# Column sums of a recurrent memory as four column tiles, with a VectorE transpose for its columns and a new order of TensorE's work

## The chip, the core and the metric

The kernel runs on one core of a Trainium2 chip. The metric is device time in microseconds of one execution of the whole program. Each version is timed several times and the median counts. The profile is of one execution, and its span runs from the first to the last recorded instruction.

The core's engines run in parallel, each through its own list of instructions, and wait for each other by semaphores: TensorE (PE in the profile, its weight loads PEld), VectorE (DVE), ScalarE (ACT), GpSimd (POOL) and SyncE (SP), which issues DMAs.

## What is computed

Four blocks in a row on x of 2048 rows by 448 columns: attention with a recurrent memory, a gated MLP, and both once more, each behind a layer norm and added to x. The attention goes through 64 segments of 32 rows, and the first 8 output rows of each segment are the memory that the next segment sees:

```python
mem = mem0
for s in range(n_seg):                       # 64 segments of 32 rows
    h = jnp.concatenate([mem, xs], axis=1)   # 8 + 32 rows, 448 wide
    q, k, v = h @ Wq, h @ Wk, h @ Wv         # 16 heads of 256
    p = softmax(mask(q @ k.T * scale))
    o = (p @ v) @ Wo                         # 40 rows, 448 wide
    mem = o[:, :M, :]
    outs.append(o[:, M:, :])
```

The MLP is `(relu(x @ W_gate) * (x @ W_up)) @ W_down` with 1792 hidden columns.

## The kernel before

**Products of weights.** At the start Wq and Wk are multiplied into one matrix A per head (`self.A`), Wv and Wo into B (`self.Bsb`), so that a segment needs U = A h, scores = U h, Y = P h and an output product with B only. `product` makes these; the "tails" among them have 64 rows each.

**Shapes of the PE array.** A matmul may use the full array (128*128 in the profile's rows, `mode=0`) or a part of it, a tile, several at a time: four column tiles (128*32, mode 1), two row tiles (64*128 or 40*128, mode 2), two column tiles of 64 (mode 3), or eight tiles 64*32 (mode 4). `packed` makes a full-shape matmul, or in mode 1 four column tiles that together give the same output. The planner has a constant, `TURN = 94.0`, for a change of shape.

**Steps.** `chain(step)` is one step of the recurrence, for both attention layers at once: the second runs `LAG = 7` steps behind the first, which makes 70 steps (0 to 69). In order:

1. `board` and `put` copy rows of other segments into spare columns of `mT` (POOL), where they ride along with the memory's columns. `mT` holds the new memory with its 448 values along the partitions, in seven blocks; keys `MEM` stand for blocks 0 to 3 and `(q, v)` for blocks 4 to 6, which hold the same values with the halves of the partitions exchanged ("cross").
2. U pass: two halves of 56 matmuls, mode 4 (line 1012), out of `mT`; copies to `Usb`, and `turn_u` transposes them on DVE into `uT`.
3. `middle`: scores (line 1208, full shape), softmax, transposed probabilities, Y in `y_part` (mode 2), and a copy to `YTm`.
4. Output pass: 56 matmuls in mode 1 (line 1051), 14 rounds of four column tiles, into one PSUM bank. Each of the four groups of 32 partitions holds a partial sum.
5. `Ohi` (ACT, line 1057) and `Olo` (DVE, line 1058) split that bank into a high and a low bf16 part.
6. Column sums: `cols` adds the four groups of partitions with the 0/1 matrix `Sel`, for both parts: eight full-shape matmuls of 32 columns, with the part of O as weights. The result has the memory's values along the partitions, and is copied to `mT` (DVE line 1074, and two cross copies), which the next step's U pass waits for. A copy `mC` and a DVE transpose (line 1078) make the rows `Rsb` of it.
7. The rows go to HR, for the first layer by POOL or ACT, for the second by DMAs on SP's queue, and those that rode along to `Tsb`.

**The rest of the work** fills the waits of the steps: `att_group` (the 32 rows of each segment that are no memory, a tile of four segments and two pairs of heads at a time: U in mode 2, scores, softmax, Y in mode 2, output products in full shape), the MLP (`glu_units` in mode 2, `glu_down` in full shape), and the norms.

**The order.** The program is a list of operations with their data dependences. `_Sched` gives each an engine and a place. PE's order is written out: `line` reads the string `LINE`, in which each character says how many of the operations still left are passed over. `ORDER` shifts the priority of groups of work on the other engines. Where an operation may take several shapes (`also`), `line` picks one that a stretch of neighbours has in common. `schedule` then plays the order through with estimated times to choose engines and banks, and `emit` writes the instructions and the semaphore waits.

Of the kernel before, what the change touches and what calls it, by code (L numbers as in the profile page):

```python
# [32 lines left out]
ORDER = ("PSaaaaoQzANGSamSAqSOLgAjolycvdUSYubSjbQxCm0psRrSRqEQAEnlIEnOAnPCTSLvPxprWKjnhTaqcrTbZCswsbraAgEaqhIaAGAaALbjaa"  # L33
         "sanTnaBcjaZWzaJKmBaaXOEYXNydtHhPuFSLsyxCuyLuORxJMA0ahaaaFcaCcCvwXmrCfR0DWCgxLBrdmbxaQC0WbaUaEGMqHa0DaosbzhpHdl"
         "WkxycjZaZGxZqQpRM0ymgeScKWuIhXaOAasLNeddFpYkHiTiewgm0WJdepBgztdDKNbipxTsJXOvpslMHKEJoVF00rXwoFGIgKaPjatRPDMuea"
         "g0ocaSMXMaIHQHYDVIDWUiVpGLFgUWXOXqRxiOaWPavfkRxbMdhxgqVYFcSAGpXxSgSAEoXcmvzKKkjJCubDis0XTbcCEuecPXEaPRWQeAORyo"
         "JHhakKaiTmlTpwUptdvkZzUD0fxNPEIziGGTevefmecgNBN0DbQOXaXPaAmfqX0pgSyloPBzIlSQcPTyKhKNWzyvrlHQFAzEIJHKDUe0hkIbfK"
         "e0zD0jsbXGXRaiTdSsamBaeyJqncMKdUTzoxjiugtllgtXxAOALDuUTVXDuwEnupSkNUaUmawjrAwhD0DLNHNtfvqgTZoJlYEDPE0EZYVTJvcw"
         "EWPEtyVNLdZeXmtsDsbxjxMTLchWdCebHajealMjeS0QOmzx0LdAHUaEDleLVrtMnIfHVmwOA0EhlPYqbAQaAoapqAIHThuLPPZmvFxkxWJWwQ"
         "nEPIcOmfgwjXdgAMZuOQkyGNViZI0sZuymZOvStgcYkKYfqeaObatwrfJE0nvRNpbkVuY0SHuqRQoFc0GZT0TAAAfPCDMqpctjaEJaZjWJfdTh"  # L40
         "pHAVWmuFXanPYnQtwEtlLmIiYjsjNpFtBblupwRveZkzOaajmjvuMshnoltlMqsanwaRPeaHaMBoa0oEtmAB0nvHQJTbpphEIqwVCbhqCNIIvN"
         "AaBEaVyVScpWtpFgRMIevwqgYYmNw0vrMkcmKEiy0rhMbriPOmkQrdu0rJkQJhZJIygthcqDsRiWahXPahhdmy0flKddE0aaaaaamLhuKetaaa"
         "aaaaaaaaaaaaaaaajYGwUNxZaCChYbrM")

SIGNS = "ABCDEFGHIJKLMNOPQRSTUVWXYZabcdefghijklmnopqrstuvwxyz0123456789+-*/=<>()[]{}.,:;!"
LINE = ("AAAABAAJAAHHCEDCCBAAIHBADCAAAAAIIEFBBABAAAHICCEAABAAAHIEDAAAAABAIHBAEBCAAAAJHADCBAAAJAAKHGBBCDAAAAfhAfACOABArZ"
        "ABAQVAUDA~QARAQAkPAFMALAAJWABHAGAcAADACARBAbWFBEADPAECMDAEQKGAAPEOOGEAEDAIDCABBDABAAWAAAKAJBAOdAGSAZAEPEEAAAKE"
        "BOACCbbF*FZAAXDGVAUUUAASADCPPAAAMAAKlKsKAJJAIAHHAAFAADACABBBWBBAMSYAAWeAJbUAJILAVKKAAAEEADGAbaGFCCAVFBZBSACQAA"
        "ANNNAAMLALvLA1KQCJIICHHHAHGGGGAcFAAACHCBAAAAXBCAAMAAXXAPGbAHSAXHGAAASDBCDABBBbaEBADCAETZAARCCPAANNNAALAMM54ALJ"
        "sJJCIBHHHAHGAHHeAGADAJDCCAAAAABCAATMBAXWeKcLKTAYMveAtALbKAAAEEAjHTA65GuGCI0C5ABxwAveeFkEqqqIApAAmAEEkkAAAhBmBX"  # L50
        "KdPAba6aaaKJCLWAVWWCAASZSAAAPADNgDQMMMjOGLALLGbJTJAOWAHDZNhGXMMGGGAGQAEAHtsDRHGAnAHAkLoHiGAgggAOAdGAedbAAAZAAd"
        "XAA2VUAAARRRtAQzQRRCDBBABAKAAAHALGFfFFFAHADAAPBCCaZBRLBVbKBZBxIBBBFTHAAXDACDC)(FpFFC[C-ABBD7BA5WCB222AT1AzAAyy"
        "QVdAuUzashqqBgoooACmAlmmMLAiAhMBBkeAdCAAaaaDaKaYQDXXrEpEVAGAYAQQYQWEEOOOHQAALGFY77JAAGA92AFKADxWwOEDtttAFKrApA"
        "qpoENDAkAAJhACf-CCdddeAADaACCZZAAADVbASARuRtRkAQQQGBACBAAKJAWcAAAffmFSdFARQfEE2AACOAYfKNBzBKIMBBBFFBEBA=/EdDC>"
        "9CEZAB4BB2kAaAyyyAyAwRAVuukjzArapEoPADlAAnAiiiJiAgAffDAOUbAgAvZ2Z0ZZZGAaYAWBqAVVD1TCAREAAOTDCqMSMMMPLAADIA33WD"
        "UCzFA3YAvQEDs~HEDqqqGqACnCnnClCCAiADPAAdCBbAeDZZZDDAAVAXWAAATRoRuRWArQEEBCBAAJJJAAAGAATEfYFldEjFEaOAAABbL6KBwB"
        "L1MLBBBLnMLBUEiB=/DACCH8CAB5+A4mED111A1AzUAyyYAAvAbssirQuAZoooADmConAAljBJiAggAACAAfbbbDbFAYZAYYEhDBVAEZAARCPW"
        "PGCNNNAALLKAC+9IPP6AHBA2L6B0RAyyyzPxACxwDUtTCrAREAnIrm;DDkkkAAEhhAihE4DeAdFAAAZCCXAAAAASSSBAhoGCBAABAAIAAAAETZ"
        "gGneSGGRQAAXCDABNYBwBWIBBByIHFBIEAA(>GgFIC-N>CAaB6An4mE222AA0Az10AZxAwA1AdtQ:s.QUApppqAOFBlMllBCAAhAmAIAdAbbSH"
        "GYYYJaEEVAXWACATAAaPWQAOOFBMMMEUATKJA77qQIe3CA7AFzSyZBAvvvAABsAttAAJoQoAAsAAkFii.BAggghD<DDAcAEADDZYAAAVAAASXR"  # L60
        "mRkAQQQCEABCAAJEAWAbAAgTeTlTGAUZAAEDRzayQBMCQLLrCKRBB2K0KBBBAEuPAHDDA44E~XECCCUyCCA1vXAtVsssRQ~CqAPoppBDuPmDAk"
        "ZiBhYAfffXfFBcBdcAAGZBBBcWAUUuDtCFRRRGFAANPAMFMMW2AAaKJDmIdIbDOHHHLLIAFFAvuAOArCAFAnBrAlNCCiiiAiAgDIAeeD{cCAaA"
        "DeAXAWCBATTTAASRASRxQoQAlEAEMALBAAIIIAIDGAUAAYDmmEQbQaQEEAdAVCAN4AAuAKzKAAAEEAsDGA//hGFC9<HdAB5GA3mE111AAzA00A"
        "UAvDvAAty0QrriqqqAZoFOAAAjnmBiiTCMgmAfAddjAAAaaaIHQcXApWaZW)WAWAbAcUMSSG6GGPPPAAONAGWW8GKATAIAQVHDOGNNNOAAAMKA"
        "MMECHJAGAFFaFAEEEAADCAAPAJGbASBAPWDIDIHAJABNBAFCADDBFKAAACCAAAAADBAFAEEFEEEADAC")


class _Op:
    __slots__ = ("idx", "engs", "cost", "fn", "deps", "prio", "dma", "eng", "ndep", "users", "ready",
                 "start", "end", "need_inc", "val", "clock", "slot", "seq", "alloc", "mode",  # L70
                 "touch", "busy", "cross", "at", "also", "land", "side", "group")


class _Bank:
# [9 lines left out]
    def ap(self):  # L84
        return self.psum[self.name][:, :]


class _Sched:
# [14 lines left out]
    LAND = 2400.0  # L103
    ROWS = {"act": 122.0, "dve": 115.0}
# [89 lines left out]
    def line(self):  # L194

        left = [o for o in self.ops if "pe" in o.engs]
        out = []
        k = 0
        for c in LINE:
            if c == "~":  # L200
                k += 80
                continue
            out.append(left.pop(k + SIGNS.index(c)))
            k = 0
        out += left
        run, have = [], None
# [10 lines left out]
    def schedule(self):  # L217
        for o in self.ops:
# [34 lines left out]
        while left:  # L253
# [209 lines left out]
UT = ["uT00", "uT01", "uT10", "uT11"]  # L463
# [91 lines left out]
MEM = [("mT", c) for c in range(2)]  # L555

# [12 lines left out]
class _Kernel:  # L569
# [48 lines left out]
    def alloc(self):  # L618
# [63 lines left out]
        self.Ohi = sb("Ohi", [128, 512])  # L682
        self.Olo = sb("Olo", [128, 512])
        self.mT = sb("mT", [128, 7, 80])
# [23 lines left out]
    def constants(self):  # L708
# [40 lines left out]
        for o in range(4):  # L749
            dve(lambda E, o=o: E.tensor_copy(self.Usb[:, 128 * o:128 * o + 128].rearrange("p (h q) -> p h q", h=H),  # L750
                                             self.ident[:, 8 * o:8 * o + 8].unsqueeze(1).to_broadcast([128, H, 8])),
                r=["ident"], w=[("Usb", o)])
            s.add("pe", 30, lambda E, e, o=o: E.matmul(mb.ap()[:, L * o:L * o + L], lhsT=self.Usb[:, 128 * o:128 * o + 128],
                                                       rhs=self.maskb[:, :], start=True, stop=True),
                  r=[("Usb", o), "mask"], w=[mb], alloc=[mb] if o == 0 else ())
# [3 lines left out]
        pool(lambda E: E.memset(self.YTm[:, :, :], 0.0), w=[("YTm", c) for c in range(2)] + [("YTr", c) for c in range(2)])  # L759
# [3 lines left out]
        pool(lambda E: E.memset(self.Usb[:, :], 0.0), w=[("Usb", r) for r in range(4)])  # L763
        pool(lambda E: E.memset(self.uT[:, 3], 0.0), w=[("uT2", a, b) for a in range(2) for b in range(2)])
        pool(lambda E: E.memset(self.mT[:, :, :], 0.0), w=MEM + ["mTr", "mT3"])
# [18 lines left out]
    def weights(self):  # L784
# [42 lines left out]
        def product(dst, terms, w, mode, scale=None, swap=False):  # L827
# [3 lines left out]
            def fn(E, e):  # L831
                for to, of in ((0, slice(64, D)), (D - 64, slice(0, 64))) if swap else ((0, slice(0, D)),):
                    for et in range(2):
                        for lhs, m0, mn, rhs, row0, _ in terms:
                            i = E.matmul(bk.ap()[row0:row0 + mn, to:to + of.stop - of.start], lhsT=lhs[:, et, m0:m0 + mn], rhs=rhs[:, et, of],  # L835
                                         start=(et == 0), stop=(et == 1), tile_position=(0, row0))
                return i
            s.add("pe", mm_cost(D, D), fn, r=[k for q in terms for k in q[5]], w=[bk], alloc=[bk], room=w, mode=mode)
# [58 lines left out]
        def values(part):  # L897
            for n in range(4 * part, 4 * part + 4):
# [11 lines left out]
                product(self.Bsb[:, b_tail(p), :], tails, [("B", p, hh, 3) for hh in range(2)], 3)  # L910
# [47 lines left out]
    def chain_start(self, c):  # L958
# [8 lines left out]
        for to, of in ((slice(0, 3), slice(0, 6, 2)), (slice(3, 4), slice(7, 8)), (slice(4, 7), slice(1, 6, 2))):  # L967
            s.add("dve", 200, lambda E, e, to=to, of=of: E.tensor_copy(self.mT[:, to, 8 * c:8 * c + 8], self.mT0[:, of, 0:M]), r=["mT0"], w=[("mT", c)], prio=0)
# [14 lines left out]
    def chain(self, step):  # L983
# [11 lines left out]
        late = []  # L995
        if ride:
            self.board(*ride)
        if third:
            u, q, o = third
            self.put(u, slice(q, q + 1), o, 32, "mT3")  # L1000
        first = 8 if third else 0

        for half in range(2):
            ub = [self.bank("C", "G") for _ in range(2)]

            def fn(E, e, half=half, ub=ub):
                for b in range(7):
                    for j in range(4):
                        for v in range(2):
                            rw = slice(64 * v, 64 * v + 64)  # L1010
                            cols = self.A[rw, b, 1792 * half:1792 * half + 1792].rearrange("p (m j i) -> p m j i", j=4, i=32)[:, :, j]
                            i = E.matmul(ub[v].ap()[32 * j:32 * j + 32, 0:D], lhsT=self.mT[rw, WHERE[b], first:first + 32], rhs=cols,  # L1012
                                         start=(b == 0), stop=(b == 6), tile_position=(64 * v, 32 * j))
                return i
# [643 lines left out]
```

## Time and profile before

| | us |
|---|---|
| median of 3 runs | 1483.35 |
| lowest and highest | 1481.13, 1483.98 |
| profiled execution | 1483.32 |
| its span | 1481.4 |
| granted TensorE clock | 1.00 |

A row of the timeline has the start, the time until the last end in it, engine, line, operation, what it writes and from what, and shapes; of a matmul the array shape (rows*columns) comes first, then partitions by columns of the moving operand. Rows of equal operations in a row are merged, with their number (x56). What stands in brackets is the engine's idle time before it and what ended it. The end of a matmul is modelled and has the pipeline's length in it, so the rate of matmuls is read from starts. A row of the stretches has the stretch, its length, then for PE, PEld, DVE, ACT and POOL the busy time and (x) the number of instructions, then the granted clock, the DMA share and GB/s. `L493` is the line in `packed`, which several operations share; their tiles tell them apart (`Sel` for the column sums, `P` for output products of attention or MLP).

### The profile page before, as it was taken

What the parts mean: (1) busy time and instruction counts of PE and PEld (TensorE: products, weight loads), DVE (VectorE), ACT (ScalarE), POOL (GpSimd) and SP (SyncE); (2) the same over time, 40 slices, a digit from 0 to 9 for tenths busy, and PEclk for the clock granted to TensorE, in tenths of its full rate; (3) what the DMA queues carried; (4) which work ended last, traced back from release to release, by engine and by line L of the source; (5) the groups of instructions that cost most, each with busy time, mean ns of one, the idle gap of its engine ahead of it and who ended that gap; (6) DMA issues with size and microseconds to landing.
All of it is one profiled execution on the core that took longest, in us unless ns stands there. A gap on an engine that the chain in (4) does not pass through costs nothing.

```text
span 1481.4 us, 79079 instructions
## 1 busy us (share of the span) xinstructions
PE 1470.8 (99%) x35068; PEld 1040.5 (70%) x35068; DVE 1136.3 (77%) x3743; ACT 925.1 (62%) x2659; POOL 176.0 (12%) x678
## 2 busy tenths in 40 slices
PE   9999999999999999999999999999999999999999
PEld 6556767676767776767768767777667776777676
DVE  6667778788877877687877878587786878688875
ACT  7765757676666666566666656575665656556643
POOL 3010111111110111011110111011110111110000
PEclk9999999999999999999999999999999999999999
DMA  9512100000000000000000000000000000000000
GB/s 267 161 31 66 50 8 9 8 9 8 9 4 16 6 11 11 4 18 4 18 4 11 12 11 12 4 18 5 18 4 11 11 11 12 5 11 5 11 5 15
DMA packets 62246, 33.85 MB, mean 23 GB/s; under 512 B 31809, under 2 KB 61777, under 8 KB 61905
## 3 DMA queue, kind: packets, MB, share of 16 engines
q1 hardware_dynamic: 61584, 28.54, 7.6%
q8 instruction: 276, 4.52, 1.3%
q14 instruction: 66, 0.53, 0.1%
q10 hardware_dynamic: 320, 0.26, 0.1%
HBM read 21.36 MB, written 1.84 MB: 16 GB/s over the span
## 4 chain that ended last, share of the span: by engine, by line
PE 97%; DVE 1%; ACT 1%; issue 0%; DMA 0%; POOL 0%; SPq 0%
PE psG L493 24%; PE psG L1354 17%; PE psC L1051 12%; PE psC L1012 9%; PE psG L1457 9%; PE psG L1012 4%; PE psG L835 3%; PE psG L1266 3%; PE psG L1486 3%; PE psG L1380 3%; PE psC L493 2%; PE psC L1208 1%; PE psC L1266 1%; PE psG L821 1%; PE psG L1051 1%; PE psG L1269 1%
## 5 line engine op out<-in xcount | busy, mean ns | idle before, releaser
L1354 PE MATMUL psG<-HT,A 64*128 64x128 bf16 x4904 | 285.9, 216 | 0.9 <-issue 0.9
L493 PE MATMUL psG<-Bsb,P 128*128 128x448 bf16 x1288 | 276.2, 353 | 0.0
L1354 PE MATMUL psG<-HX,A 64*128 64x128 bf16 x3678 | 267.0, 216 | 0.4 <-issue 0.4
L1354 PEld LDWEIGHTS psG<-HT,A 64*128 64x128 bf16 x4904 | 235.2, 94 | 11.6 <-issue 3.7
L483 ACT ACTIVATE Ug<-psG 64x128 bf16<-64x128 f32 (+2 forms) x447 | 158.9, 372 | 60.0 <-PE psG L1354 43.9
L1354 PEld LDWEIGHTS psG<-HX,A 64*128 64x128 bf16 x3678 | 194.7, 94 | 1.4 <-issue 1.4
L1051 PE MATMUL psC<-Bsb,YTm 128*32 128x448 bf16 x3528 | 178.8, 353 | 0.4
L493 PEld LDWEIGHTS psG<-Bsb,P 128*128 128x128 bf16 x1288 | 110.7, 97 | 94.7 <-issue 11.9
L1012 PE MATMUL psC<-A,mT 64*32 64x448 bf16 x3920 | 152.8, 350 | 0.2
L1012 PE MATMUL psG<-A,mT 64*32 64x448 bf16 x3920 | 152.1, 350 | 0.0
L1192 DVE STREAM_TRANSPOSE uT<-Usb 128x384 bf16<-128x384 bf16 x280 | 144.1, 536 | 0.0
L1051 PEld LDWEIGHTS psC<-Bsb,YTm 128*32 128x32 bf16 x3528 | 88.7, 97 | 70.8 <-issue 2.5
L1457 PE MATMUL psG<-GG,glu 64*128 64x256 bf16 x2352 | 134.2, 269 | 0.0
L1457 PEld LDWEIGHTS psG<-GG,glu 64*128 64x128 bf16 x2352 | 111.9, 94 | 17.0 <-issue 1.9
L486 DVE CAST Ug<-psG 64x128 bf16<-64x128 f32 (+2 forms) x260 | 107.6, 424 | 15.5 <-PE psG L1354 10.7
L1012 PEld LDWEIGHTS psC<-A,mT 64*32 64x32 bf16 x3920 | 78.7, 92 | 57.2 <-ACT mT L483 5.2
L483 ACT ACTIVATE P<-psG 128x448 bf16<-128x448 f32 x210 | 106.4, 545 | 8.6 <-PE psG L1269 7.1
L486 DVE CAST P<-psG 128x448 bf16<-128x448 f32 x148 | 89.1, 614 | 12.7 <-PE psG L1269 11.2
L493 PE MATMUL psG<-glu,P 128*128 128x448 bf16 x448 | 97.6, 352 | 0.0
L1468 DVE TENSOR_TENSOR P<-P,psG 128x512 bf16<-128x512 bf16 x84 | 57.6, 686 | 44.5 <-ACT P L1467 44.0
L1012 PEld LDWEIGHTS psG<-A,mT 64*32 64x32 bf16 x3920 | 79.4, 92 | 17.4 <-issue 0.7
L1058 DVE TENSOR_TENSOR Olo<-psC,Ohi 128x448 bf16<-128x448 f32 x65 | 40.4, 622 | 64.3 <-ACT Ohi L1057 63.8
(253 smaller groups left out, 3025.2 us busy)
## 6 DMA issues: line engine op xcount, KB each, us to landing
HR<-xn SPq DMA_DIRECT2D x128, 32.0 KB, 1.9
Tsb<-Rsb SPq DMA_DIRECT2D x256, 1.5 KB
Tsb<-Rsb SPq DMA_DIRECT2D x256, 2.0 KB
Bsb<-in_A_Wq_dram SPq DMA_DIRECT2D x6, 384.0 KB, 7.3
Bsb<-in_A_Wk_dram SPq DMA_DIRECT2D x6, 384.0 KB, 6.2
HR<-Rsb SPq DMA_DIRECT2D x126, 1.5 KB
HR<-Rsb SPq DMA_DIRECT2D x126, 2.0 KB
X<-in_A_x_dram SPq DMA_DIRECT2D x16, 112.0 KB, 3.1
```

The costliest lines, as they stand in the source:

```text
L483: return E.activation(out, i, ACT.Copy, scale=1.0 if scale is None else scale)
L486: return E.tensor_copy(out, i)
L493: return E.matmul(out, lhsT=lhsT, rhs=rhs, **k)
L835: i = E.matmul(bk.ap()[row0:row0 + mn, to:to + of.stop - of.start], lhsT=lhs[:, et, m0:m0 + mn], rhs=rhs[:, et, of], start=(et == 0), stop ...
L1012: i = E.matmul(ub[v].ap()[32 * j:32 * j + 32, 0:D], lhsT=self.mT[rw, WHERE[b], first:first + 32], rhs=cols, start=(b == 0), stop=(b == 6), ...
L1051: x = E.matmul(bo.ap()[32 * j:32 * j + 32, 0:D], lhsT=self.YTm[:, q, :], rhs=self.Bsb[:, chunks[q], :], start=(i == 0), stop=(i == 13), ti ...
L1192: self.s.add("dve", 560, busy=486.0, fn=lambda E, e, v=v, of=of: E.transpose(outs[:, 2 * v:2 * v + 2], of), r=[("Usb", 2 * half + v)], w=[ ...
L1266: return E.matmul(ps[:, n * q:n * q + n], lhsT=HR[rows, 128 * q:128 * q + 128], rhs=PT, start=True, stop=True, tile_position=(b, 0))
L1354: i = E.matmul(ub[v].ap()[:, 128 * n:128 * n + 128], lhsT=self.A[rw, b, a0:a0 + 128], rhs=HT[rw, WHOLE[b], :, 0:SEG] if CROSS[b] is None e ...
L1380: i = E.matmul(psS()[:, sg, :], lhsT=Ug[:, k, sg, :], rhs=HT[:, k, sg, :], start=(k == 0), stop=(k == 3))
L1457: i_ = E.matmul(two[v].ap()[:, 256 * c:256 * c + 256], lhsT=self.Wgu[rw, b, f0:f0 + 128], rhs=self.GG[rw, :, WHOLE[b] if CROSS[b] is None ...
L1468: s.add("dve", dv_cost(512), lambda E, e, z=z, dst=dst: E.tensor_tensor(dst, dst, z(1), ALU.mult), r=[two[1]], w=w)
```

## The change

In steps 16 to 60 (`EARLY <= step < LATE`) the column sums exchange their operands: `Sel` is the weight, O is streamed, and four column tiles each take one set of 32 columns of every block, for the high part and then the low. Their result has the memory in rows. It is copied to `R`, which was the result of the transpose before, and a DVE transpose of `R` writes the columns straight into `mT`; the cross copies read `mT` in place of PSUM. In the next step the memory stands in columns 16 to 31 of `mT` and what rides along in 0 to 15 (`swap`). The other steps keep the old sums.

```diff
+        if turn:
+            def cols(E, e):
+                for q, O in enumerate((hi_, lo_)):
+                    for j in range(4):
+                        x = E.matmul(br.ap()[32 * j:32 * j + 32, 0:128], lhsT=self.Sel[:, :], rhs=O[:, 64:576].rearrange("p (k i) -> p k i", k=4)[:, :, 32 * j:32 * j + 32],
+                                     start=(q == 0), stop=(q == 1), tile_position=(0, 32 * j))
+                return x
+            s.add("pe", mm_cost(128, 128), cols, r=ok + ["Sel"], w=[br], alloc=[br], room=[rk], mode=1, **P)
+            s.add(EV, ev_cost(128), copy_any(R[:, :], lambda: br.ap()[:, 0:128]), r=[br], w=[rk], **P)
+            s.add("dve", 307, busy=225.0, fn=lambda E, e: E.transpose(self.mT[:, 0:4, m0:m0 + 32], rows), r=[rk], w=MEM + LAST + ["mT3"], **P)
+            for v, (to, of) in enumerate(((low, upp), (upp, low))):
+                s.add(EV, ev_cost(48, fast=True), copy_any(self.mT[to, 4:7, m0:m0 + nm], self.mT[of, 0:3, m0:m0 + nm]), r=MEM, w=xk(v), at=2 + v, side=v, **P)
+        else:
...
-            s.add("pe", mm_cost(*[D] * (hi - lo)), oo, r=yk + bk, w=[bo], alloc=[bo] if (g == 0 and lo == 0) else ())
+            s.add("pe", mm_cost(*[D] * (hi - lo)), oo, r=yk + bk, w=[bo], alloc=[bo] if (g == 0 and lo == 0) else (), also=(1,))
```

The last pair is in `att_group`; the products of `glu_down` and the tails of B get `also=(1,)` in the same way, so that they may be made as four column tiles where a neighbour is. `Ohi` and `Olo` become 576 wide, with the first 64 columns repeated behind the 448 twice instead of once.

The U pass is cut, so that a part may start when the part of `mT` that it reads is there, and in steps 0 to 15 half 1 is copied and transposed in two halves of 224 columns; Y goes to two banks where the first layer alone is running:

```diff
+            split = (((0, 2, 4), MEM), ((1, 3, 5, 6), cross + LAST + LASTX)) if swap else (((0, 2), MEM), ((1, 3), cross), ((4, 5, 6), LAST + LASTX))
+            for bs, mk in split if (early or swap) and half == 0 else whole:
...
+            for gs in ((0,), (1,)) if early and half == 1 else ((0, 1),):
+                n = 224 * len(gs)
...
+        two = len(act) == 1 and c1 == 1 and m["n"] == "m"
+        yb = [self.bank("C", "G") for _ in (0, 1)] if two else [self.bank("C", "G") for _ in act]
```

In the planner, an operation takes the shape of the one behind it where that is its plain shape, and the estimate of PE's time includes a supply of instructions (`FETCH` ns for each, with a lead of at most `AHEAD`):

```diff
+        for a, b in zip(out[-2::-1], out[:0:-1]):
+            if a.mode != b.mode == plain[a.idx]:
+                a.mode = b.mode
...
+                lead = min(self.AHEAD, lead + t0 + c - free[e] - o.ins * self.FETCH[self.FETCH[2] < t0 < self.FETCH[3]])
+                c -= min(lead, 0.0)
+                lead = max(lead, 0.0)
```

`ORDER` and `LINE` are new strings.

More of the change, by code (lines that the diff above doesn't have):

```diff
@@ L1003, in chain @@
+        cross = [(q, v) for q in MEM for v in range(2)]
+        whole = (((0, 1, 2, 3, 4, 5, 6), MEM + cross + LAST + LASTX),)
         for half in range(2):
             ub = [self.bank("C", "G") for _ in range(2)]
[L1006 to L1014, printed above, removed]
@@ L1078, in chain @@
[L1078 removed]
+        low, upp = slice(0, 64), slice(64, 128)
+        nm = 8 if step < LAG else 16
+        ok = [("Ohi", 0), ("Oli", 0), "Oh2", "Ol2"]
+        xk = lambda v: [(q, v) for q in MEM] + [("mTc", v)]
+        br = self.bank("C", "G")
+        rows = R[:, :].rearrange("p (k i) -> p k i", k=4)
+        turn = EARLY <= step < LATE
```

287 lines of the change are left out of this document (171 added, 116 removed).

## The prediction

> **What bounds the kernel now.** I read the page's engine shares and its chain first, then busy time by stretches, then the timeline of one step.
>
> ```profile
> span 1481.4 us, 79079 instructions
> PE 1470.8 (99%) x35068; PEld 1040.5 (70%) x35068; DVE 1136.3 (77%) x3743; ACT 925.1 (62%) x2659; POOL 176.0 (12%) x678
> PE 97%; DVE 1%; ACT 1%; issue 0%; DMA 0%; POOL 0%; SPq 0%
> ```
>
> TensorE is busy for 99% of the span and is 97% of the chain that ended last. The recurrence (70 steps, each using the memory that the step before wrote) isn't what limits the time as long as the order puts other tiles' matmuls into each of its waits. The stretches say where that succeeds:
>
> ```profile
> 0.00:60.00 60.00, 57.93 (x851) 39.31 (x853) 42.62 (x95) 44.51 (x76) 14.37 (x43) 1.00 0.91 260
> 60.00:342.00 282.00, 278.10 (x7018) 190.45 (x7014) 212.27 (x715) 186.75 (x528) 34.96 (x134) 1.00 0.10 25
> 342.00:1262.00 920.00, 918.53 (x22094) 654.36 (x22096) 720.55 (x2418) 576.88 (x1724) 109.48 (x433) 1.00 0.05 10
> 1262.00:1432.00 170.00, 169.82 (x4084) 120.56 (x4069) 131.39 (x440) 99.19 (x291) 16.23 (x67) 1.00 0.04 8
> 1432.00:1481.40 49.40, 46.45 (x1054) 35.86 (x1052) 29.42 (x79) 17.73 (x44) 0.99 (x3) 1.00 0.05 13
> ```
>
> The second number is PE's busy time. From 342 to 1262 us PE idles 1.47 of 920 us: a microsecond of PE work taken out there is a microsecond of the span. These are also, within a step, the steps 16 to 60, for which the change rewrites the column sums. From 60 to 342 us (steps 0 to 15) PE idles 3.9 us. The clock is granted in full (1.00) throughout.
>
> Busy PE time contains more than streaming. One step, from its output pass to the next U pass:
>
> ```profile
> 834.84 2.83 PE L1051 MATMUL psC<-Bsb,YTm 128*32 128x448 bf16 x56
> ...
> 837.60 1.12 PE L493 MATMUL psG<-Bsb,P 128*128 128x448 bf16 x5
> 837.72 0.54 ACT L1057 ACTIVATE Ohi<-psC 128x448 bf16<-128x448 f32 x1 [1.38 <-PE psC L1051]
> ...
> 838.30 0.62 DVE L1058 TENSOR_TENSOR Olo<-psC,Ohi 128x448 bf16<-128x448 f32 x1 [0.67 <-ACT Ohi L1057]
> ...
> 838.62 1.11 PE L493 MATMUL psG<-Bsb,P 128*128 128x448 bf16 x5
> ...
> 838.97 0.17 DVE L1060 COPY Olo<-Olo 128x64 bf16<-128x64 bf16 x1
> ...
> 839.56 0.18 PE L493 MATMUL psC<-Sel,Ohi 128*128 128x32 bf16 x1
> 839.59 0.18 PE L493 MATMUL psC<-Sel,Olo 128*128 128x32 bf16 x1
> ...
> 839.74 0.18 PE L493 MATMUL psC<-Sel,Olo 128*128 128x32 bf16 x1
> ...
> 839.77 0.28 PE L513 MATMUL psG<-ident,Px 128*128 128x64 bf16 x4
> ...
> 839.88 0.92 PE L493 MATMUL psG<-Bsb,P 128*128 128x448 bf16 x4
> 839.96 0.23 DVE L1074 CAST mT<-psC 128x64 bf16<-128x64 f32 x1 [0.81 <-PE psC L493]
> ...
> 840.38 0.20 ACT L483 ACTIVATE mT<-psC 64x48 bf16<-64x48 f32 x1
> ...
> 840.61 0.28 ACT L483 ACTIVATE mC<-psC 128x128 bf16<-128x128 f32 x1
> 840.73 0.09 PEld L1012 LDWEIGHTS psC<-A,mT 64*32 64x32 bf16 x1 [0.37 <-ACT mT L483]
> 840.73 0.36 PE L1012 MATMUL psC<-A,mT 64*32 64x448 bf16 x1
> ...
> 840.75 0.09 PEld L1012 LDWEIGHTS psG<-A,mT 64*32 64x32 bf16 x1
> 840.75 0.36 PE L1012 MATMUL psC<-A,mT 64*32 64x448 bf16 x1
> ...
> 840.92 0.31 DVE L1078 STREAM_TRANSPOSE Rsb<-mC 128x128 bf16<-128x128 bf16 x1 [0.17 <-ACT mC L483]
> 840.93 0.35 PE L1012 MATMUL psC<-A,mT 64*32 64x448 bf16 x1
> ```
>
> The third column of a row (the first number after the time) includes a pipelined tail, so I use differences of start times. Five products of 448 columns in full array shape run from 838.62 to 839.56: 0.188 us each. Four of the same start at 839.88, which should free PE at 840.63, but the U pass, of another array shape (64*32), starts at 840.73: **a change of shape costs 0.10 us**. It is the same at the output pass: 14 sets of four column tiles (128*32) fill 834.84 to 837.60, 2.76 us; 14 times 0.190 is 2.66, and the rest is the change to the full shape. So a set of four column tiles of 448 columns costs the same as one full product of 448 columns.
>
> **The change part by part.** *The column sums themselves* (cols, steps 16 to 60, 45 of them). Before: eight full-shape matmuls of 32 columns from 839.56 to 839.77, 0.21 us, which is 26 ns each. After: two rounds (high and low part) of four column tiles of 128 columns. The trace has no such matmul in column shape. From below, four tiles stream together, as the U pass does, where the first and the last of eight tiles start at 840.73 and 840.75 and the next round only at 840.93 (0.19 us for 448 columns): scaled to 128 columns that is 0.054 us a round, 0.11 in all. From above, each of the eight is paid at the 26 ns of the old ones: 0.21, no gain. I take 0.11, since eight starts within 0.02 us show that a tile isn't charged 26 ns. Gain 0.10 x 45 = **4.3 us**, at least 0.
>
> The Trainium skill (TensorE: Matmul & The Clock Gate, section "Wait — 56ns, not 53.3ns?") says that matmul starts are never closer than about 25 ns, however few columns they stream; by that the eight tiles would take 0.20 us as before and the sum below would come out 4.3 us later. The old sums agree with it (26 ns), the tiles of the U pass do not (840.73 to 840.75).
>
> *The changes of shape around them.* Before, the path from output pass to U pass is column shape, full (the cover and the sums), then 64*32: two changes at the least. After, the sums are in column shape, and the cover (output products of attention and GLU) may be column tiles too, so that column to 64*32, one change, is enough. What the order does now I counted in the PE timeline, over the stretch whose first and last output passes are these:
>
> ```profile
> 342.30 2.83 PE L1051 MATMUL psC<-Bsb,YTm 128*32 128x448 bf16 x56
> ...
> 1255.24 2.83 PE L1051 MATMUL psC<-Bsb,YTm 128*32 128x448 bf16 x56
> ```
>
> In these 45 steps there are 130 changes of shape between output pass and next U pass (21 steps have two, 15 have three, the rest more). At one each, 85 go: 8.5 us at 0.10. At no change of the order's habits, none go. I take 65, since every step has at least one to lose, and steps with a row-shaped piece in between will not lose all: **6.5 us**. The cover needs 9 to 10 products before the sums and 4 to 5 after them. The supply:
>
> ```profile
> L493 PE MATMUL psG<-Bsb,P 128*128 128x448 bf16 x1288 | 276.2, 353 | 0.0
> L493 PE MATMUL psG<-glu,P 128*128 128x448 bf16 x448 | 97.6, 352 | 0.0
> ```
>
> 1736 over 69 steps is 25 a step, so the 14 are there.
>
> *The chain from sums to U.* Before: sums end 839.92 (last start plus 0.18), mT copy 0.23 (L1074), cross copies until 840.58, U possible at about 840.64; the cover ends at the same moment. After, in sequence: copy of the sums out of PSUM (0.28, the mC row), transpose into mT (0.31, the Rsb row; same operation and shape), and then the first three blocks of U may start, the cross copies (0.20) being needed only by the second part. With the sums 0.10 earlier and 0.05 us for each hand-over: 839.82 + 0.05 + 0.28 + 0.05 + 0.31 + 0.05 = 840.56. Equal within 0.1 us, so **0**; if DVE is in the middle of another tile's 0.62 us copy it is up to 0.6 later, which one more covering product of each 0.19 us hides, three of them at most. Queued behind the transpose on DVE are other tiles' copies and, on POOL, the HT copies of 0.2 us, needed only after the U pass. The old mT copy (0.23 on DVE) is gone, and the rows for HR and for the SP queue's small transfers come a transpose earlier; none of these was waited for by PE.
>
> *Steps 0 to 15.* U half 0 in three pieces by the part of mT they read, half 1 copied and transposed in two halves, Y in two banks: the chain gets shorter where PE idles 3.9 us, plus waits below 0.2 us that the modelled tails hide. The smaller copies cost fixed time on ACT and DVE, neither of them full. I take **2.5 us**, between -1 (more pieces, more waits) and 6.
>
> *The planner* (instruction supply in its model, ties of shape) and the new order issue nothing. The order also moves everything else by its own luck: 0, ±4 us.
>
> Sum: 4.3 + 6.5 + 0 + 2.5 = 13.3 us off the profiled execution of 1483.32 (span 1481.4 and 1.9 around it; the median of the runs, 1483.35, is the same): **1470.0 us**.
>
> **The rivals.** *The order uses little of it*: the sums are shorter, but the cover stays row-shaped or full and only some 20 changes go: 4.3 + 2 = 6.3 us less, 1477. For it: 23 of the 45 steps have row-shaped work between output pass and U pass now. Against: no row forces it there, with 14 products a step that may take column shape.
>
> *The floor of 26 ns holds for tiles of 128 columns*: 1474.3.
>
> *The gain is given back*: the shape changes move to another place of the step (there the cover after U becomes row-shaped, and the scores, which exist in full shape only, get a change on each side: two more a step, 9 us), which leaves 1483 to 1479: no change, 1482.
>
> *Slower, by the cover after U.* This is the one place where the same products are needed twice:
>
> ```profile
> 843.50 0.57 PE L1380 MATMUL psG<-HT,Ug 128*128 128x40 bf16 x16
> 843.92 2.05 PE L493 MATMUL psG<-Bsb,P 128*128 128x448 bf16 x10
> 845.81 0.36 PE L1208 MATMUL psC<-HT,uT 128*128 128x40 bf16 x8
> ```
>
> Ten of the products cover the copy and transposes of U before the step's scores (845.81). 14 and 10 are 24 of the 25 a step has. If the new order spends more of them in column shape before U, PE waits after U; at half a microsecond a step that is 22 us against 13: 1492. It decides from 0.3 us a step (13.3 / 45). Against it: the order can move a GLU or attention product of row shape there at a price of two changes, 0.2.
>
> **How the numbers follow.** Forecast 0.52 (own range 1462 to 1476), little use 0.18, floor 0.05, given back 0.10, slower 0.15. About 3 us (0.2%) is what a measurement here can tell from no change. Faster: 0.52 + 0.05 + 0.15 of the 0.18 = 0.72; within 0.2%: 0.03 + 0.10 = 0.13; slower 0.15. The range reaches up to 1486, past the given-back case and leaving out most of the slower one, and down to 1459 (8.5 + 4.3 + 6 + 4 = 23 us, with a little over).
>
> **What would show it.** In the changed trace: the sums as 128*32 matmuls of 128 columns, eight within 0.11 us from first start to next operation; output products of attention as 128*32 between output pass and sums; one change of shape between output and U pass in most of steps 16 to 60; PE busy from 342 us on still above 99%, and fewer PE microseconds per step. Wrong would be: PE waits of 0.3 us or more a step for mT or uT, the eight tiles 26 ns apart, or as many shape changes as now.

## The result, and the profile after

The changed kernel takes 1480.51 us (median of 22 runs, 1478.58 to 1483.32), the kernel before 1483.38 us beside it (22 runs, 1480.5 to 1485.45): a ratio of 0.9982, interval 0.9975 to 0.9988. It is faster, by 2.9 us where 13.3 us were forecast; the time lies inside the stated range, but that range reaches up to 1486 and so holds no change at all as well. The profiled executions show a similar step: the span is 3.6 us shorter (1481.4 to 1477.8), at the same clock. Its page starts like this, with the shares of the engines and of the chain that ended last:

```profile
span 1477.8 us, 82082 instructions
...
PE 1466.8 (99%) x36535; PEld 1043.3 (71%) x36535; DVE 1139.6 (77%) x3755; ACT 916.8 (62%) x2654; POOL 180.3 (12%) x697
...
PE 97%; DVE 1%; ACT 1%; issue 0%; POOL 0%
```

TensorE is the bound as before, and only 4.0 us less of it is busy. Where they come from is seen in stretches cut at the output passes: steps 2 to 15, 16 to 60, and the rest. First the kernel before (columns as in the prediction's stretches):

```profile
103.00:342.30 239.30, 236.42 (x6298) 167.91 (x6297) 185.78 (x645) 156.21 (x463) 29.73 (x117) 1.00 0.11 27
342.30:1272.60 930.30, 928.84 (x22337) 661.02 (x22334) 729.37 (x2449) 583.96 (x1743) 110.97 (x438) 1.00 0.05 10
1272.60:1481.40 208.80, 205.66 (x4872) 149.51 (x4871) 151.69 (x486) 109.71 (x314) 15.74 (x63) 1.00 0.04 9
```

Then the changed kernel:

```profile
102.80:341.40 238.60, 235.36 (x6295) 166.91 (x6294) 188.96 (x658) 154.69 (x483) 34.39 (x137) 1.00 0.11 27
341.40:1266.70 925.30, 924.28 (x23642) 662.91 (x23641) 729.02 (x2440) 576.45 (x1711) 109.98 (x431) 1.00 0.05 10
1266.70:1477.80 211.10, 207.49 (x4970) 150.07 (x4962) 152.95 (x496) 108.45 (x307) 15.91 (x66) 1.00 0.04 9
```

The second column is each stretch's length: 0.7 us shorter in steps 2 to 15, 5.0 us shorter in steps 16 to 60, and 2.3 us longer behind them.

Busy time of PE cannot say what it was busy with, since the time of a change of shape counts as busy (run x2 below shows it). So I split each stretch by the starts of all matmuls: streaming (each matmul at the spacing that its shape and columns have in an unbroken row of equals, 0.188 to 0.190 us for 448 columns, divided by the tiles that run side by side), the number of changes of shape at 0.094 us (the kernel's `TURN`), and what remains, waits. Beyond the streaming of the matmuls ahead of it, a change shows as 0.09 us in both traces (0.089 to 0.096 in the median, whichever two shapes it joins), so this size is borne out. The split of streaming and waits is an estimate, good to some 0.6 us. On the other side, the planner puts filler matmuls where its estimate has PE waiting (`filler`, a full-shape product of A that nothing reads); they count as streaming here.

| | before: length, streaming, changes, waits | after |
|---|---|---|
| steps 2 to 15 | 239.3 us, 218.8 us, 121, 9.1 us | 238.6, 218.9, 114, 9.0 |
| steps 16 to 60 | 930.3, 892.2, 314, 8.5 | 925.3, 887.0, 310, 9.2 |
| from step 61 to the last matmul | 205.5, 197.2, 65, 2.2 | 207.8, 197.8, 66, 3.8 |

There are 15 fillers after and 8 before, all of them ahead of 304 us; a difference in the later stretches isn't theirs. In steps 16 to 60 the streaming fell by 5.2 us, and the number of changes hardly: 314 to 310. Between output pass and U pass alone, where the prediction counted 130, there are now 131. Not all of the 5.2 us is the sums' own: where the next matmul has the same shape, the sums take 0.204 us before and 0.121 after in the median, 0.083 us a step or 3.7 us in 45 steps. Of the rest, 0.6 us is other work that now stands behind step 61 (197.2 to 197.8), and the remainder is within the error of the split.

What the change can do shows in the timeline of step 40, all engines, some rows left out:

```profile
834.50 2.82 PE L1104 MATMUL psC<-Bsb,YTm 128*32 128x448 bf16 x56
...
837.15 1.88 PE L534 MATMUL psG<-Bsb,P 128*32 128x448 bf16 x36
...
837.95 0.62 DVE L1115 TENSOR_TENSOR Olo<-psC,Ohi 128x448 bf16<-128x448 f32 x1 [2.17 <-ACT Ohi L1114]
...
838.61 0.20 DVE L1119 COPY Olo<-Olo 128x128 bf16<-128x128 bf16 x1
...
838.86 0.24 PE L1134 MATMUL psC<-Ohi,Sel 128*32 128x128 bf16 x4
...
838.92 0.23 PE L1134 MATMUL psC<-Olo,Sel 128*32 128x128 bf16 x4
...
838.98 1.88 PE L534 MATMUL psG<-Bsb,P 128*32 128x448 bf16 x36
839.20 0.28 ACT L520 ACTIVATE Rsb<-psC 128x128 bf16<-128x128 f32 x1 [0.95 <-PE psC L1134]
...
839.51 0.31 DVE L1139 STREAM_TRANSPOSE mT<-Rsb 128x128 bf16<-128x128 bf16 x1 [0.71 <-ACT Rsb L520]
839.86 0.37 DVE L523 COPY mT<-mT 64x48 bf16<-64x48 bf16 x2
...
840.78 0.76 PE L1060 MATMUL psC<-A,mT 64*32 64x448 bf16 x24
```

Here output pass, cover (nine products, each four column tiles: 838.86 - 837.15 = 1.71 us, 0.190 each), sums and cover again are all 128*32, and one change is left, ahead of the U pass: 838.98 plus nine times 0.190 is 840.69, and the U pass starts at 840.78. The sums themselves take 838.86 to 838.98. But the U pass follows in one change in only 11 of the 45 steps. In the step ahead of that one, PE's rows read:

```profile
814.86 2.83 PE L1104 MATMUL psC<-Bsb,YTm 128*32 128x448 bf16 x56
817.63 0.34 PE L1351 MATMUL psG<-PTx,HR 40*128 40x128 bf16 x6
...
819.43 0.22 PE L544 MATMUL psG<-ident,Px 64*128 64x64 bf16 x4
819.59 0.24 PE L1134 MATMUL psC<-Ohi,Sel 128*32 128x128 bf16 x4
819.65 0.23 PE L1134 MATMUL psC<-Olo,Sel 128*32 128x128 bf16 x4
819.71 1.12 PE L534 MATMUL psG<-Bsb,P 128*32 128x448 bf16 x20
820.76 0.34 PE L1351 MATMUL psG<-PTx,HR 40*128 40x128 bf16 x6
...
821.32 0.76 PE L1060 MATMUL psC<-A,mT 64*32 64x448 bf16 x24
```

Column, row, column, row, eight tiles: four changes. Sums in full shape between the same neighbours would have as many. Most of the cover is row-shaped work, and only five products in column shape are spent behind the sums. Row-shaped work stands between output pass and U in 29 of the 45 steps, and by the same count in 24 before (the prediction has 23): the new order put more of it there. Over the whole program the output products are split like this:

```profile
L530 PE MATMUL psG<-Bsb,P 128*128 128x448 bf16 x966 | 205.9, 352 | 0.2 <-issue 0.2
...
L534 PE MATMUL psG<-Bsb,P 128*32 128x448 bf16 x1512 | 80.4, 353 | 0.0
...
L530 PE MATMUL psG<-glu,P 128*128 128x448 bf16 x336 | 72.7, 352 | 0.0
...
L534 PE MATMUL psG<-glu,P 128*32 128x448 bf16 x392 | 21.0, 353 | 0.0
```

1512 and 392 column tiles make 476 products, against 1302 in full shape: 27% are in column shape. Counted by place in the 45 steps, there are 27.9 products a step: 11.6 between output pass and U (8.5 of them in column shape), 5.2 from U to the scores, and 11.2 between scores and the next output pass, of which all but one a step are full.

### The profile page after: what moved, and what is told of

The parts are those of the page before. It is cut to its first block, busy times and chain, and to the rows that moved or that the text cites. A ratio compares the mean times of both kernels' runs of the same rounds, so it can differ in the third digit from the quotient of the medians.

```text
span 1477.8 us, 82082 instructions
## 1 busy us (share of the span) xinstructions
PE 1466.8 (99%) x36535; PEld 1043.3 (71%) x36535; DVE 1139.6 (77%) x3755; ACT 916.8 (62%) x2654; POOL 180.3 (12%) x697
## 4 chain that ended last, share of the span: by engine, by line
PE 97%; DVE 1%; ACT 1%; issue 0%; POOL 0%
PE psG L530 18%; PE psG L1439 17%; PE psC L1104 10%; PE psG L1542 9%; PE psC L1060 7%; PE psG L534 6%; PE psG L1060 5%; PE psG L877 3%; PE psG L1351 3%; PE psG L1571 3%; PE psG L1465 3%; PE psG L1104 2%; PE psC L1351 1%; PE psC L1290 1%; PE psG L861 1%; PE psC L1439 1%
## 5 line engine op out<-in xcount | busy, mean ns | idle before, releaser
L530 PE MATMUL psG<-Bsb,P 128*128 128x448 bf16 x966 | 205.9, 352 | 0.2 <-issue 0.2
L520 ACT ACTIVATE Ug<-psG 64x128 bf16<-64x128 f32 (+2 forms) x422 | 150.0, 372 | 52.5 <-PE psG L1439 37.6
L1104 PE MATMUL psC<-Bsb,YTm 128*32 128x448 bf16 x3136 | 159.3, 353 | 0.0
L1060 PE MATMUL psG<-A,mT 64*32 64x448 bf16 x4116 | 133.3, 350 | 0.0
L530 PEld LDWEIGHTS psG<-Bsb,P 128*128 128x128 bf16 x966 | 83.6, 97 | 67.9 <-issue 5.2
L523 DVE CAST Ug<-psG 64x128 bf16<-64x128 f32 (+2 forms) x289 | 118.4, 419 | 16.9 <-PE psG L1439 11.7
L1060 PE MATMUL psC<-A,mT 64*32 64x448 bf16 x3724 | 125.0, 350 | 0.3 <-DVE mT L523 0.3
L520 ACT ACTIVATE P<-psG 128x448 bf16<-128x448 f32 x226 | 114.6, 544 | 10.1 <-PE psG L1354 9.1
L1060 PEld LDWEIGHTS psC<-A,mT 64*32 64x32 bf16 x3724 | 62.1, 92 | 47.0 <-DVE mT L1139 3.5
L523 DVE CAST P<-psG 128x448 bf16<-128x448 f32 x132 | 80.0, 615 | 12.7 <-PE psG L1354 10.6
L1060 PEld LDWEIGHTS psG<-A,mT 64*32 64x32 bf16 x4116 | 68.7, 92 | 28.1 <-issue 1.0
L1552 ACT ACTIVATE P<-psG 128x512 bf16<-128x512 f32 x83 | 49.4, 595 | 60.1 <-PE psG L1542 51.6
L534 PE MATMUL psG<-Bsb,P 128*32 128x448 bf16 x1512 | 80.4, 353 | 0.0
```

Source lines behind the costliest of these rows:

```text
L520: return E.activation(out, i, ACT.Copy, scale=1.0 if scale is None else scale)
L523: return E.tensor_copy(out, i)
L530: return E.matmul(out, lhsT=lhsT, rhs=rhs, **k)
L534: i = E.matmul(out[q], lhsT=w, rhs=rhs, tile_position=(0, 32 * j), **k)
L1104: x = E.matmul(bk.ap()[32 * j:32 * j + 32, c0:c0 + d1 - d0], lhsT=self.YTm[:, q, :], rhs=self.Bsb[:, chunks[q], d0:d1], start=(i == 0), st ...
L1552: s.add("act", ev_cost(512)["act"], lambda E, e, dst=dst, z=z: E.activation(dst, z(0), ACT.Relu), r=[two[0]], w=w, room=old)
```

## The experiments

Two questions were open: which of the four terms was worth how much, and why the changes of shape stayed. The first four runs take parts of the change away, the next three take away the cuts and the planner's supply, and the last one forces what the prediction had assumed. Spans, of one execution each, are compared with the changed kernel's 1477.8; the ratios are to the kernel before, timed beside each group of runs (medians 1482.43 us for x1 to x4, 1481.83 for x5 to x7, 1482.00 for x8). By the ratios the differences to the changed kernel come out between 0.2 us smaller and 1.3 us larger than by the spans.

**Old sums under the new order** (x1). Steps 16 to 60 get the eight full-shape matmuls back, and the text of everything else stays:

```diff
-        if turn:
-            def cols(E, e):
...
-        else:
-            def cols(E, e):
...
+        def cols(E, e):
+            for k in range(4):
+                for q, O in enumerate((hi_, lo_)):
+                    x = packed(E, e, br.ap()[:, 32 * k:32 * k + 32], O[:, 64 + 128 * k:192 + 128 * k], self.Sel[:, :], start=(q == 0), stop=(q == 1))
+            return x
```

> The changed kernel with its own order, but the column sums of steps 16 to 60 in the old form (eight full-shape matmuls of 32 columns, three copies from PSUM, transpose for the rows afterwards). Theory A: the column tiles of the sums are worth their streaming time, 45 x 0.10 = 4.3 us, and keep some shape changes away; the instruction list of this kernel has 554 shape changes against 546, 0.8 us. So 1480.5 + 5 = 1485.5, 1484 to 1489. Rival: the sums lie beside other work and their length does not count: 1480 to 1481.

Measured: 1489.02 us, ratio 1.0046 (1.0031 to 1.0061), span 1486.5, 8.7 us over the changed kernel. Steps 16 to 60:

```profile
342.10:1276.50 934.40, 930.55 (x22531) 664.29 (x22529) 731.74 (x2451) 583.52 (x1739) 109.93 (x437) 1.00 0.05 10
```

One thing more changes with it. The products may still be made as column tiles, but with full-shape sums beside them `line` makes most of them in full shape again, and all of those between output pass and U in these steps:

```profile
L530 PE MATMUL psG<-Bsb,P 128*128 128x448 bf16 x1278 | 271.8, 353 | 0.0
...
L534 PE MATMUL psG<-Bsb,P 128*32 128x448 bf16 x264 | 14.7, 354 | 0.0
```

Steps 16 to 60 are 9.1 us longer than with the new sums: 5.2 of streaming (892.2 against 887.0), eight more changes, and 3.2 of waits. The streaming has four fillers in it (0.8 us) that the changed kernel doesn't have there; what is left, 4.4 us, is about the sums' own 3.7. The time is at the upper edge of what was expected. So the new order is built around the new sums: with old sums it is slower than the old order.

**New sums and new order, products in full shape only** (x2). `also=(1,)` is removed in all three places:

```diff
-            s.add("pe", mm_cost(*[D] * (hi - lo)), oo, ..., also=(1,))
+            s.add("pe", mm_cost(*[D] * (hi - lo)), oo, ...)
```

> The changed kernel with its own order, but all output products of attention and MLP and the tails of B in full (or 64-column) shape as before; the new sums stay. The instruction list then has 641 shape changes instead of 546. Theory A: each costs 0.095 us, so 9 us more: 1489.5, 1487 to 1492; the products in column shape then do not save changes against before, they only pay for those that the new sums bring. Rival: the changes fall where PE would wait anyway, under 2 us: 1480.5 to 1482.5.

Measured: 1490.48 us, ratio 1.0055 (1.0040 to 1.0070), span 1488.0. The whole program has 641 changes of shape, against 546 with column products and 555 before; its streaming is the changed kernel's to 0.1 us. So 95 changes and what comes with them cost 10.2 us, **0.107 us each**; at the 0.094 us of a change alone they make 8.9 us, and the other 1.3 are waits. Steps 16 to 60:

```profile
343.80:1277.60 933.80, 932.97 (x22369) 656.05 (x22364) 730.44 (x2443) 576.03 (x1708) 110.06 (x431) 1.00 0.05 10
```

PE's busy time rises with the length, from 924.28 to 932.97: this is what changes of shape look like in the profile, busy time and no idle time. In these steps there are 392 of them, 82 more than in the changed kernel and 78 more than before. The three kernels with the new order give the balance without the order in it. Between output pass and U there are 139 changes with the old sums (x1), 202 with the new sums and full products (x2), and 131 with column products too. This is the balance that the prediction missed: column-shaped sums alone *bring* changes, 63 here, since they part from the full-shape cover; the column products take these back, and eight more.

**Old order, new sums and column products** (x3). `ORDER` and `LINE` of before, U uncut, the cuts of steps 0 to 15 off, no supply in the planner:

```diff
-            for bs, mk in split if (early or swap) and half == 0 else whole:
+            for bs, mk in whole:
...
-            for gs in ((0,), (1,)) if early and half == 1 else ((0, 1),):
+            for gs in ((0, 1),):
...
-        two = len(act) == 1 and c1 == 1 and m["n"] == "m"
+        two = False
```

> The old order (both strings), with the new sums and products that may be column tiles, U pass and early steps uncut as before. Theory L: the path from the sums to the U pass is longer (copy, transpose, cross copies one after the other, all of them needed before an uncut U), and the old order's cover of 0.85 to 1 us is too short, so PE waits 0.2 to 0.4 us before U in most of the 45 steps, 9 to 18 us; with 601 shape changes instead of 555 (4 us more) and the sums shorter (4 us less): 1492 to 1501. As predicted (path no longer than before): no waits, 1483 to 1484.

Measured: 1505.83 us, ratio 1.0157 (1.0142 to 1.0172), span 1502.5: worse than the expectation allowed. Steps 16 to 60, and what TensorE's weight loads for the U pass sat idle for (sum and number of times):

```profile
342.30:1291.90 949.60, 940.28 (x22945) 661.25 (x22943) 729.61 (x2427) 576.69 (x1726) 111.11 (x433) 1.00 0.05 10
```

```profile
  ACT mT L519: 9.0, 19
  DVE mT L522: 6.3, 12
```

(The second fence is of the whole run.) The 19.3 us over before are 366 changes instead of 314 (4.9 us), waits of 22.4 us instead of 8.5, and 0.6 us of streaming: what the new sums save is eaten by fillers, 32 in all where before has 8, and 23 of them in this stretch. The waits are for the cross copies: they read `mT`, so they come behind the transpose, and an uncut U pass needs them. The shortest time from the end of the sums to the U pass is 1.20 us here, 0.85 before, and 0.90 in the changed kernel, whose U pass may start on the first three blocks.

**Old order, old sums, columns of `mT` exchanged** (x4). As x3, with the sums of x1 and without `also`; what is left of the change is that memory and riding rows change places in `mT`, and the wider `Ohi` and `Olo`.

> The old order and the old sums, uncut U pass and early steps; only the places of memory and riding rows in mT are exchanged in steps 17 to 61, as the change does. If the exchange costs nothing: 1483.4 within 1.5. If the riders' copies or the transition of the places at steps 16 and 61 make the U pass wait: 1485 to 1488.

Measured: 1485.4 us, ratio 1.0022 (1.0010 to 1.0034), span 1483.6. The split shows 314 changes and 892.5 us of streaming in steps 16 to 60, as before, and 0.4 to 0.8 us more waits in each of the three stretches. So the exchange is no gain, and 2.2 us of loss by the span (3.3 by the ratio), as the second case of the expectation had it; it is a condition of the new sums, since the transpose writes blocks of 32 columns.

**U pass waits for all of `mT`** (x5), in steps 17 to 61:

```diff
-                s.add("pe", mm_cost(*[D] * len(bs)), fn, r=mk + held + ...
+                s.add("pe", mm_cost(*[D] * len(bs)), fn, r=(whole[0][1] if swap else mk) + held + ...
```

> The changed kernel with its own order; the only edit: in steps 17 to 61 the first part of the U pass waits for all of mT, as the second part does, so that the cross copies stand ahead of it. Theory L: the path of the new sums is longer by the cross copies that follow the transpose, and the cut of the U pass is what keeps it off PE; where the cover is at its shortest (0.90 to 1.05 us, some 14 of 45 steps) PE then waits 0.2 to 0.35 us, and part of that is lost: 4 to 8 us, 1484.5 to 1488.5. As predicted (path equal to the old within 0.1 us, only with the cut): the same. Rival: the cut does nothing, 1480 to 1481.5.

Measured: 1486.02 us, ratio 1.0027 (1.0018 to 1.0036), span 1483.2, 5.4 us over the changed kernel. The waits of TensorE's weight loads by what they wait for (total, times, longest), steps 16 to 60:

```profile
PEld psC L1060 <- DVE mT L523: 4.6, 11, 0.6
PEld psC L1060 <- ACT mT L520: 4.1, 7, 0.8
```

In the changed kernel the same view has

```profile
PEld psC L1060 <- DVE mT L1139: 3.5, 9, 0.4
...
PEld psC L1060 <- DVE mT L523: 1.3, 4, 0.4
...
PEld psC L1060 <- ACT mT L520: 0.5, 2, 0.3
```

Without the cut, U waits for the cross copies (L520, L523), with it for the transpose (L1139). Steps 16 to 60 are 7.1 us longer: 14.2 us of waits in place of 9.2, seven fillers more (1.3 us), seven changes; the end is 1.0 us shorter. The cut is worth more than the new sums' streaming: without it the change is a loss.

**The cuts of steps 0 to 15 undone** (x6):

```diff
-                s.add("pe", mm_cost(*[D] * len(bs)), fn, r=mk + held + ...
+                s.add("pe", mm_cost(*[D] * len(bs)), fn, r=(whole[0][1] if early else mk) + held + ...
...
-            for gs in ((0,), (1,)) if early and half == 1 else ((0, 1),):
+            for gs in ((0, 1),):
...
-        two = len(act) == 1 and c1 == 1 and m["n"] == "m"
+        two = False
```

> The changed kernel with its own order; undone: in steps 0 to 15 the pieces of the U pass wait for all of mT, half 1 is copied and transposed whole, and Y goes to one bank. Theory A: the early cuts are worth what was predicted, 2.5 us: 1483. Theory E: the new order leans on them, so without them it loses more than the change gained by them, 4 to 6 us: 1484.5 to 1486.5. Rival: nothing, 1480 to 1481.5.

Measured: 1484.32 us, ratio 1.0016 (1.0007 to 1.0026), span 1481.9. It falls between the two theories, nearer to E's range than to A's 1483. Steps 2 to 15, and there the largest wait for the cross copies and the largest for Y's copy:

```profile
104.00:345.80 241.80, 235.74 (x6294) 166.89 (x6297) 189.37 (x650) 152.23 (x454) 30.39 (x118) 1.00 0.10 27
```

```profile
PEld psC L1060 <- ACT mT L520: 1.8, 4, 0.7
...
PEld psC L1104 <- ACT YTm L520: 1.1, 3, 0.6
```

The stretch is 3.2 us longer than in the changed kernel (238.6), all of it waits (12.4 against 9.0), with the same streaming and the same 114 changes. Yet before, without any cut, it had 9.1 us of waits. So the new order leans on the cuts: without them it waits more than the old order did, with them as much. The 3.2 us stand clear of chance: four other kernels with the new order and the cuts (x1, x2, x5, x7) take 237.9 to 239.8 us for this stretch.

**No supply of instructions in the planner** (x7), which changes only its estimate, and by it the choice of engines and banks:

```diff
-                c -= min(lead, 0.0)
+                c -= 0.0
```

> The changed kernel with its own order, but without the supply of instructions in the planner's estimates: the same PE order, other choices of engines and banks in places. Expected by all: 1480.5 within 2 us; if it is 3 us or more slower, the new estimates carry a part of the gain.

Measured: 1479.69 us, ratio 0.9987 (0.9977 to 0.9996), span 1478.2, with the changed kernel's streaming and changes in steps 16 to 60 (887.0 us, 310). Its interval and the changed kernel's (0.9975 to 0.9988) overlap, and the spans differ by 0.4 us: no difference that can be told.

**Products forced into the path** (x8). In eight steps (16, 29, 33, 36, 44, 47, 53, 56) only `LINE` is changed: row-shaped work between output pass and U pass moves ahead of the output pass, and products that stood between the scores and the output pass move behind it in its place, in column shape. One piece of it:

```diff
-        "MCvCABysAjqbHoAnnAAlADUmkkiAASgMBBdBhAba8IZZZIAAWJBJVVVASASAXAIPANNhDQMMMGMiGGJAJJJaTIAHNAUkGaZGAJKVJJJFFFAADD"
+        "MCvCABysAjqbHHYmAllAAjAmkkiAASgMBBdBhAba8IZZZIAAWJBJVVVASASAXAIPANNhDQMMMGMiGGJAJJJaTIAHNAUkGaZGAJKVJJJFFFAADD"
```

> The changed kernel, only its PE order edited: in eight steps (16, 29, 33, 36, 44, 47, 53, 56) the row-shaped work between output pass and U pass is moved ahead of the output pass, and output products from between the scores and the output pass are moved behind it, in column shape. The instruction list has 539 shape changes instead of 546. Theory P, as predicted: only the changes count, 7 x 0.095: 0.7 us less, 1479.8. Theory S: the products cover a wait where they are, and the row-shaped work delays the output pass where it goes, so the recurrence comes late by 1 to 2 us in each edited step: 8 to 16 us more, 1488 to 1497, as waits of PE in steps 16 to 60 and not as streaming.

Measured: 1495.43 us, ratio 1.0086 (1.0069 to 1.0103), span 1493.4: 15.6 us slower than the changed kernel, with eight steps edited. Steps 16 to 60, then waits of the weight loads there:

```profile
344.20:1283.10 938.90, 929.27 (x23639) 663.79 (x23639) 727.08 (x2430) 575.99 (x1712) 108.52 (x426) 1.00 0.05 10
```

```profile
PEld psC L1134 <- DVE Olo L1119: 5.2, 15, 0.9
PEld psC L1060 <- DVE mT L1139: 4.6, 11, 0.7
...
PEld psG L1351 <- ACT PTx L520: 2.2, 2, 1.1
```

The changes did fall, 310 to 303, which is 0.7 us. The stretch idles 9.6 us (938.90 - 929.27) where the changed kernel idles 1.0 (925.30 - 924.28), and the split has 21.3 us of waits for 9.2. Streaming is 2.1 us more there, which is fillers (all in this stretch, 20 of them more) less what was moved ahead of its first output pass:

```profile
L1607 PE MATMUL psG<-A 128*128 128x448 bf16 x35 | 8.6, 353 | 0.0
```

The waits are of several kinds: the row-shaped work, brought forward, waits for its own inputs (`PTx`, up to 1.1 us), and the sums and the U pass wait longer for theirs (up to 0.9 and 0.7 us, where the changed kernel has 0.4 at most). The products had covered something where they stood. Steps with fewer changes can be written; these eight, placed like this, cost far more than they save. The edit moves row-shaped work and products at once, so the run doesn't say how much of the loss belongs to which.

## Why the prediction was right and wrong

**What bounds the kernel: right.** Time follows PE's starts in every run. Whatever lengthened streaming, added changes or added waits came back in the span.

**The column sums, 4.3 us: right.** The sums take 0.12 us (838.86 to 838.98) where 0.11 was taken and 0.21 stood before; in the median it is 0.121 for 0.204, which makes 3.7 us, and x1 loses about as much. (0.10 x 45 is 4.5, not 4.3; both are close.) The rule of the Trainium skill weighed there (TensorE: Matmul & The Clock Gate, section "Wait — 56ns, not 53.3ns?") would have made the eight tiles 0.20 us; the trace disagrees for tiles that run side by side. The rival "floor of 26 ns" is out.

**The changes of shape, 6.5 us: this is the step that failed.** "I take 65, since every step has at least one to lose" of the 85: none went there (130 to 131), and four went in the whole stretch, 0.4 us in place of 6.5. Two things were wrong in it. First, the 130 were taken as a stock from which column products subtract. In the new order there are 139 with the old sums (x1), the new sums first add 63 by parting from the full-shape cover (x2), and column products then take 71. The baseline for that term was the kernel with new sums, in its own order, not the kernel before. Second, "1736 over 69 steps is 25 a step, so the 14 are there" counted products and not when they are ready or what they cover. There are 28 a step, but 16 of them stand from U to the next output pass, and what the path got, 8.5 in column shape a step, leaves row-shaped work around the sums in most steps (29 of 45). x8 tried the assumption: products and row-shaped work moved in eight steps cost 15.6 us for seven changes. It is not shown that every other placing costs as much; no better order was run, so whether one exists stays open.

The size of 0.10 us for one change was right (0.09 by the gaps in the traces, 0.107 by x2 with the waits that came along).

**The path from sums to U, 0: right, and resting on one edit.** "Equal within 0.1 us" was 1.06 before (0.21 and 0.85) against 1.02 after (0.12 and 0.90). The prediction named the cut of the U pass in one clause; x5 prices it at 5.4 us, and in x3, with the uncut path, waits rose by 13.9 us, more than the whole forecast gain. Weight loads do wait for the transpose, 3.5 us in nine waits, but loads run ahead of their matmuls (the cover of step 40 loads from 836.96 and multiplies from 837.15): waits as a whole rose by only 0.7 us, which the split can't tell from nothing.

**Steps 0 to 15, 2.5 us: no gain shown.** Steps 2 to 15 are 0.7 us shorter in the profiled execution (239.3 to 238.6), but x1, x2, x5 and x7, with the same order and cuts there, take 237.9 to 239.8, on both sides of before. The cuts are worth 3.2 us under the new order (x6), but without them that order waits 3.3 us more than the old one.

**Planner and order, 0 ±4: within it.** The planner's supply does nothing (x7). The changed kernel is 2.3 us longer behind step 61, where hardly any part of the change but the order and the products' shape is at work: 1.6 us of waits more and 0.6 of streaming. That the order costs this isn't shown. From step 61 to the last matmul, before takes 205.5 us and the changed kernel 207.8; the six other kernels with the new order there (x1, x2, x5 to x8) take 206.6 to 207.3, and x4 and x3, with the old order, 206.4 and 207.3.

**The sum as it came out:** streaming 5.2 + changes 0.4 - waits 0.7 in steps 16 to 60, + 0.7 in steps 2 to 15, + 0.2 ahead of them, - 2.3 at the end, 3.6 us of span (0.1 is rounding). Counted over the whole program instead of by stretches, the sums give 3.7 us, nine changes fewer 0.8, and seven fillers more take 1.3; the 0.4 left over are not told apart. By this count what the change gained is about what the sums gained, and the two terms added to them, changes of shape and early steps, came to little.

**The rivals.** "Little use of it" had the right reason, row-shaped cover, but let 20 changes go and came to 1477. "Given back" had 1482, the nearest number, but not the mechanism: in 7 of the 11 steps with one change most of the cover after U is row-shaped, but so it is in 24 of all 45 steps, and in 28 before. And the rest of a step didn't get more changes (4.09 to 3.98 a step); the gain was not moved elsewhere, it never arose. The slower rival, waits behind U for want of cover, did not occur in the changed kernel, where 5.2 products a step still stand from U to the scores (5.6 before); x8, which takes products from between scores and output pass instead, and moves row-shaped work too, lost more than it won.

## What to carry to other kernels

When a piece of work changes its array shape, count the changes of shape of the kernel with that piece alone altered, and let the neighbours' new freedom subtract from that, not from the count of today. A supply of filler counted per step says nothing yet: list where each filler stands, what it covers there, and from when it is ready, because in a kernel whose engine is 99% busy, like this one, a filler may already be someone's cover (x8). And where a path is longer by a copy and a transpose, an edit that lets the consumer start on part of the data can decide the sign of the whole change.

## What the runs showed of the hardware

A change of array shape costs 0.09 us between the starts of two matmuls (0.089 to 0.096 in the median for each pair of shapes), 0.107 us with everything around it (95 changes, 10.2 us), and appears as busy time of PE, not as idle time. The Trainium skill (TensorEngine Tiling (Array Packing), section "Key Properties") says that a change of tiling mode drains the engine; the gaps fit that, and the price is from here.

Four column tiles of 128 columns start a round every 0.06 us (838.86, 838.92, 838.98), which is 15 ns a matmul where full-shape matmuls of 32 columns are 26 ns apart. Small matmuls in tiles are here paid by the round, not by the matmul. And four column tiles of 448 columns take 0.190 us, a full product 0.188, so a product's shape can be chosen by its neighbours alone.
